# An empty planned step between a reciprocal and the scaling that reads it, with new ranks, in a planned attention and MLP-Mixer kernel

## The chip, the cores and the metric

The kernel runs on one core of a Trainium2 chip. The metric is device time in microseconds of one execution, lower is better. The profile is one execution seen by the hardware profiler; its times count from the first instruction.

## The reference

Top-32 attention for 8 batches of 8 heads, 576 rows, 64 columns a head, and behind it a token- and channel-mixing MLP. What is computed:

```python
scores = scale * np.matmul(q, k.transpose(0, 1, 3, 2))
kth = np.partition(scores, -top_k, axis=-1)[..., -top_k:-top_k + 1]
scores = np.where(scores >= kth, scores, -1000000000.0)
scores = scores - np.max(scores, axis=-1, keepdims=True)
attn = np.exp(scores)
attn = attn / (np.sum(attn, axis=-1, keepdims=True) + 1e-09)
x = np.matmul(attn, v)                      # heads laid side by side: 576 x 512 a batch
u = x + (np.maximum(x.T @ w_tok1, 0) @ w_tok2).T
out = u + np.maximum(u @ w_ch1, 0) @ w_ch2
```

## The kernel before

Work is cut into 32 units; a unit is one pair of heads of one batch, so four units make a batch. A unit's scores are nine tiles of 128 rows by 576 columns, in two groups: group 0 has four tiles, group 1 five.

**Through the engines.** TensorE makes scores, ScalarE copies them to SBUF (`SS`). VectorE finds the 32nd largest value of each row: `upper` (L428) takes the larger of two halves, `split4` (L452, L456, L460) halves again, `top_round` runs MAX8 and MATCH_REPLACE8 in rounds (L473, L478), and `low_round` (L492) ends the search. GpSimd meanwhile makes the smaller halves by integer arithmetic (`both_bits` L435, `lower_bits` L443). From the result, `raise_kth` (L544) makes `kbig`, which ScalarE needs for a steep ReLU (L550); GpSimd's `sink` (L558) subtracts it from the scores, and ScalarE's exponential follows (L532); those tiles are turned by DMA transposes (L563). The other tiles are turned on TensorE (L582, L585). In the last group of the last unit VectorE masks directly (`kept`, L574).

**Output of the attention.** For each head (`hh` 0 or 1), TensorE multiplies by v with a column of ones beside it (`o_mm`, L650), so that the row sums come out as a 65th column. VectorE takes their reciprocal (`o_den`, L662). Then the product is scaled: on ScalarE in five pieces (`o_ev`, L672), or on VectorE in one instruction (`o_ev_dve`, L681). `DIVIDED = (0, 1)` gives VectorE the second head of every odd unit, so 16 scalings, one of them in the last unit. `h1_mm` (L692) and what follows it use the scaled result.

**The last batch.** Partial sums of the MLP's second part are made on TensorE early (`pre_mm`, L1103) and copied out, one by ScalarE and eleven by VectorE (L338). When the last unit's attention is done, the rest is added to them (L1174, L1178) and the output accumulated (L1156). VectorE also checks flags: seven parts (L1253), a reduction (L1256) and a cast (L1263).

**The order.** All of this is put down as steps of a planner (`Plan`, L40). A step has an engine, a planned duration, a priority, the steps that it depends on, the buffers that it takes and gives back, and a slack: a planned time that must pass behind its predecessor on another engine. `Plan.order` plays the steps through in planned time; whenever an engine is free it takes, of the steps that are ready, the one with the lowest priority number. Steps marked as using the port (all of GpSimd's arithmetic, and VectorE's `upper` and `split4`) aren't started while another such step runs. What comes out is only an order: each engine executes its instructions in it, and waits for data by semaphores. Priorities are 100 per unit plus an entry of `RANK` for most kinds of step. Three entries are no priorities but times in tenths of a microsecond: `o_wait` (ahead of a reciprocal, behind the output matmul), `t_wait` (behind a DMA transpose) and `q_wait` (ahead of the transposes of q and k). A step on the pseudo engine "FREE" takes no time and issues nothing; what depends on it becomes ready 0.12 us (`LAG` of VectorE) behind a VectorE step that it depends on, where a VectorE step that depends on it directly would be ready at once. `raise_kth` has had such a step ahead of it already.

Of the kernel before, what the change touches and what calls it, by code (L numbers as in the profile page):

```python
# [17 lines left out]
JOINT = 4  # L18
PRE_OF = 12
RANK = {  # L20
    "begin_l": -2054, "o_wait": 16, "t_wait": 6, "q_wait": 272, "v_wait": 112, "pre_mm": -34365, "pre_ev": -31279, "rest_mm": 14920,
    "begin": 31546, "flags": 8794, "rush": -6145, "rush6": -3394, "load": -9078, "qk_tr": 7627, "qk_ev": -3163, "st_mm": -8007,
    "st_ev": 896, "keep": 3463, "h1_mm": -30213, "h1_ev": 3666, "ut_mm": -46945, "ut_ev": -3088, "out_mm": 13329, "out_ev": -772,
# [5 lines left out]
}  # L29
SPARE_US = 0.22  # L30
LEAD = 3.0
# [8 lines left out]
class Plan:  # L40
# [9 lines left out]
    def add(self, eng, dur, prio, fn, deps=(), acq=(), rel=(), slack=0.0, port=None):  # L50
        t = Task()
        t.eng, t.dur, t.prio, t.fn, t.acq, t.rel, t.slack = eng, dur, prio, fn, acq, rel, slack
        t.succ, t.nd, t.ready, t.seq = [], 0, 0.0, len(self.tasks)
        t.port = (eng == "POOL") if port is None else port
        for d in deps:
            if d is not None:
                d.succ.append(t)
                t.nd += 1
        self.tasks.append(t)
        return t  # L60
# [88 lines left out]
def kernel(  # L149
# [494 lines left out]
    def o_mm(st, mst, p, hh, wide=False):  # L644
        PT = st["PT"]
        O = bank("mps" if wide and hh else "O")[:, 0 : NS * D1].rearrange("p (t d) -> p t d", t=NS)
        for t in range(NS):
            ms = csz(t)
            for j in range(NS):
                nc.tensor.matmul(  # L650
                    out=O[0:ms, t, :],
                    lhsT=PT[:, hh, j, t * P : t * P + ms],
                    rhs=mst["vb"][:, j, 2 * p + hh, :],
                    start=(j == 0),
                    stop=(j == NS - 1),
                )
        st["O", hh] = O

    def o_den(st, hh):
        O = st["O", hh]  # L660
        rden = denp.tile([P, NS], f32, name="rden", tag="rden")
        nc.vector.reciprocal(rden[:, :], O[:, :, D])  # L662
        st["rden", hh] = rden

    def o_ev(st, mst, hh, p):
        if "Xb" not in mst:
            mst["Xb"] = take("xb", xbufs)
        Xb, O, rden = mst["Xb"], st.pop(("O", hh)), st["rden", hh]
        c0 = (2 * p + hh) * D
        for t in range(NS):  # L670
            ms = csz(t)
            nc.scalar.activation(  # L672
                out=Xb[0:ms, t, c0 : c0 + D],
                in_=O[0:ms, t, 0:D],
                func=AF.Copy,
                scale=rden[0:ms, t : t + 1],
            )

    def o_ev_dve(st, mst, hh, p):
        O, c0 = st.pop(("O", hh)), (2 * p + hh) * D  # L680
        nc.vector.tensor_tensor(  # L681
            out=mst["Xb"][:, :, c0 : c0 + D], in0=O[:, :, 0:D],
            in1=st["rden", hh][:, :].unsqueeze(2).to_broadcast([P, NS, D]), op=ALU.mult,
        )
# [129 lines left out]
    add = pl.add  # L814
# [41 lines left out]
    def plan_unit(u):  # L856
        b, p = divmod(u, NPAIR)
        st, mst = sts[u], msts[b]
        U = 100 * u
        last = u == NU - 1  # L860
# [8 lines left out]
        for i in range(2):  # L869
# [5 lines left out]
                    deps=[a] + (ev[-1:] if u else []), rel=[("tp", u, "q", i)])  # L875
# [8 lines left out]
        kd, selE, keep, nmx, PTd = {}, {}, {}, {}, {}  # L884
# [4 lines left out]
        for g in range(2):  # L889
# [6 lines left out]
            for hh in range(2):  # L896
# [3 lines left out]
                        deps=[a] + ([] if early else evs),  # L900
# [14 lines left out]
            if g == 1:  # L915
                for part in range(2):
                    a = add("PE", (1.01, 0.28)[part], U + RANK["st_mm"], lambda part=part: st_mm(st, part),
                            deps=[smm[-1]], acq=[("s0", u, "st", part)],
                            rel=[("qkT", u)] if part else [])
# [3 lines left out]
                            deps=[a, e0] + ([evs[-1]] if part else []),  # L923
                            rel=[("s0", u, "st", part)])
# [34 lines left out]
        def to_pt(t):  # L959
            return [t, home], []  # L960

        tails = []
        for g in range(2):
# [4 lines left out]
            for i in gtiles(g):  # L968
                if i in st["turned"]:
# [11 lines left out]
                    deps, acq = to_pt(y)  # L981
# [14 lines left out]
                deps, acq = to_pt(tr)  # L996
# [3 lines left out]
                rel=[(f"SS{g}", u), ("nmax", u, g)]  # L1000
# [3 lines left out]
            for tiles in [pairs] + [[i] for i in olds if i not in pairs]:  # L1004
                if not tiles:
                    continue
                tr = add("PE", 0.14 + (0.055 if fast else 0.105) * len(tiles), V + RANK["pt_tr" + str(g)] + 4 * g, lambda tiles=tiles: ptail_tr(st, tiles),
                         deps=mains, acq=[("tp", u, "l", tiles[0])],
                         rel=[(r, u, i) for r in ("E" if fast else "EU") for i in tiles])
                deps, acq = to_pt(tr)  # L1010
                tails.append(
                    add("ACT", 0.07 + 0.1 * len(tiles), V + RANK["pt_ev" + str(g)], lambda tiles=tiles: ptail_ev(st, tiles),
                        deps=deps, acq=acq, rel=[("tp", u, "l", tiles[0])])
# [4 lines left out]
        oe, oes = None, []  # L1018
        for hh in range(2):
            wide = last and hh  # L1020
            div = wide or hh >= 2 - DIVIDED[u % 2]
            O = ("mps" if wide else "O", u, hh)
            om = add("PE", 1.01, V + RANK["o_mm" + str(hh)], lambda hh=hh: o_mm(st, mst, p, hh, last),
                     deps=[wt["v", b, t] for t in range(NS)] + [None if last else oe] + tails + [PTd[i] for i in range(NTILE) if i == 2 * NT or i % 2 == hh],
                     acq=[O], rel=([("PT", u)] if hh else []) + ([("vb", b)] if hh and p == NPAIR - 1 else []))
            r = add("DVE", 0.08, U - 500, lambda hh=hh: o_den(st, hh), deps=[om], acq=[("den", u, hh)],
                    slack=0.0 if last else (0.3 if b == B - 1 else 0.1 * RANK["o_wait"]))
            if div:
                oe = add("DVE", 0.53, U - 500, lambda hh=hh: o_ev_dve(st, mst, hh, p), deps=[r], rel=[O, ("den", u, hh)])
            else:  # L1030
                oe = add("ACT", 0.99, V + RANK["o_ev" + str(hh)], lambda hh=hh: o_ev(st, mst, hh, p), deps=[r],
                         acq=[("Xb", b)] if p == 0 and hh == 0 else [], rel=[O, ("den", u, hh)])
            oes.append(oe)
# [9 lines left out]
        for part in range(2):  # L1043
# [4 lines left out]
                    deps=[a] + mst.get("ute", [])[:1],  # L1048
# [224 lines left out]
    for u in range(NU):  # L1273
        plan_unit(u)
        if u == NU - 2:
            plan_part_sums(B - 1)
        if u == NU - 1:
            plan_mlp_last(B - 1)
        elif (u + 1) % NPAIR == 0:
            plan_mlp(u // NPAIR)  # L1280
# [6 lines left out]
    with tc.If(flag != 0):  # L1287
        with tc.For_i(0, B, 1) as bv:
            mst = {}
            for p in range(NPAIR):  # L1290
                st = {"turned": ()}
# [82 lines left out]
```

## Time and profile before

| what | value |
|---|---|
| time, median of 3 runs | 885.52 us (884.84 to 885.58) |
| the profiled execution's own time | 884.62 us |
| its span, first to last instruction | 882.8 us |
| mean granted TensorE clock | 0.999 |
| VectorE busy | 861.7 us, 98% |
| ScalarE busy | 834.1 us, 94% |
| TensorE busy | 819.8 us, 93% |
| GpSimd busy | 597.2 us, 68% |

Of the profiled execution's time, 1.8 us lie around the span. TensorE's busy time has filler matmuls in it (L277), which keep it running where it has nothing to do. In the rows quoted below, DVE is VectorE, ACT ScalarE, PE TensorE, POOL GpSimd. A row of the timeline has the start and the duration in us, the engine, the line, the operation and its tiles, and how many instructions are merged. A row of a group has the count, then the busy time in us and the mean duration in ns, then the idle time ahead of them.

### The profile page before, as it was taken

What the parts mean: (1) busy time and instruction counts of PE and PEld (TensorE: products, weight loads), DVE (VectorE), ACT (ScalarE), POOL (GpSimd) and SP (SyncE); (2) the same over time, 40 slices, a digit from 0 to 9 for tenths busy, and PEclk for the clock granted to TensorE, in tenths of its full rate; (3) what the DMA queues carried; (4) which work ended last, traced back from release to release, by engine and by line L of the source; (5) the groups of instructions that cost most, each with busy time, mean ns of one, the idle gap of its engine ahead of it and who ended that gap; (6) DMA issues with size and microseconds to landing.
All of it is one profiled execution on the core that took longest, in us unless ns stands there. A gap on an engine that the chain in (4) does not pass through costs nothing.

```text
span 882.8 us, 22107 instructions
## 1 busy us (share of the span) xinstructions
PE 819.8 (93%) x7328; PEld 468.6 (53%) x7417; DVE 861.7 (98%) x3850; ACT 834.1 (94%) x1857; POOL 597.2 (68%) x513
## 2 busy tenths in 40 slices
PE   8998988999989999999999999899989999899997
PEld 5666545455545555455554555455555455545552
DVE  8999999999999999999999999999999999999993
ACT  4999999999999999999999999999999999999953
POOL 5679776776877766686676777577667767656700
PEclk9999999999999999999999999999999999999999
DMA  9656764254233453226432552224431453111101
GB/s 129 76 93 83 97 96 77 30 86 83 57 59 42 86 84 83 30 42 121 64 58 38 66 110 57 58 38 90 79 77 31 54 110 55 23 32 43 56 19 58
DMA packets 207483, 58.93 MB, mean 67 GB/s; under 512 B 199809, under 2 KB 202305, under 8 KB 207361
## 3 DMA queue, kind: packets, MB, share of 16 engines
q1 hardware_dynamic: 164320, 48.33, 27.2%
q0 software_dynamic: 40560, 8.46, 11.8%
q8 instruction: 60, 0.98, 0.5%
q10 hardware_dynamic: 2480, 0.66, 0.4%
q14 instruction: 63, 0.51, 0.2%
HBM read 35.78 MB, written 9.44 MB: 51 GB/s over the span
## 4 chain that ended last, share of the span: by engine, by line
ACT 52%; DVE 28%; PE 13%; issue 4%; POOL 2%; DMA 1%; SPq 0%; DVEq 0%; ACTq 0%
ACT SS L336 10%; DVE A L473 7%; ACT E L532 7%; DVE hx L478 6%; ACT U L567 6%; ACT U L550 6%; ACT pb L532 5%; PE mps L788 4%; DVE A L492 4%; ACT pt L605 4%; ACT H2T L754 4%; DVE hi L428 3%; ACT xb L672 3%; ACT qkT L336 2%; DVE hx L460 2%
## 5 line engine op out<-in xcount | busy, mean ns | idle before, releaser
L435 POOL TENSOR_TENSOR lo<-SS 128x1152 int32<-128x1152 int32 x64 | 168.8, 2638 | 241.8 <-DVE A L473 178.0
L473 DVE MAX8 A<-hx 128x8 f32<-128x72 f32 (+2 forms) x1152 | 270.1, 294 | 0.0
L478 DVE MATCH_REPLACE8 hx<-A,hx 128x72 f32<-128x72 f32 (+1 forms) x864 | 199.4, 242 | 0.0
L336 ACT COPY SS<-s 128x512 f32<-128x512 f32 x379 | 171.7, 527 | 5.5 <-PE s L389 5.2
L443 POOL TENSOR_TENSOR lo<-lo,hi 128x1152 int32<-128x1152 int32 x64 | 168.7, 2636 | 0.0
L389 PE MATMUL s<-qkT 64*128 64x512 f32 x508 | 161.6, 640 | 0.4 <-ACT SS L336 0.4
L558 POOL TENSOR_TENSOR SS<-SS,U 128x576 f32<-128x576 f32 x126 | 158.6, 1275 | 0.0
L532 ACT ACTIVATE E<-SS,nmax 128x576 bf16<-128x576 f32 x162 | 129.0, 824 | 1.8 <-POOL nmax L518 1.7
L582 PE MATMUL tp<-identB,E 128*128 128x128 bf16 (+1 forms) x785 | 117.4, 221 | 11.0 <-ACT pt L609 7.6
L567 ACT ACTIVATE U<-SS,A 128x576 bf16<-128x576 f32 x157 | 126.7, 837 | 0.0
L585 PE MATMUL tp<-identN,U 128*128 128x128 bf16 (+1 forms) x785 | 112.7, 220 | 9.9 <-ACT U L567 9.0
L492 DVE MAX8 A<-lo 128x8 f32<-128x296 f32 x288 | 116.9, 452 | 0.0
L550 ACT ACTIVATE U<-SS,kbig 128x576 bf16<-128x576 f32 x126 | 100.0, 822 | 4.0 <-DVE kbig L544 4.0
L788 PE MATMUL mps<-wc2b,H2T 128*128 128x512 bf16 (+1 forms) x402 | 101.9, 380 | 1.9 <-issue 1.4
L532 ACT ACTIVATE pb<-SS,nmax 128x576 bf16<-128x576 f32 x126 | 99.5, 814 | 4.2 <-POOL SS L558 4.0
L585 PEld LDWEIGHTS <-U 128*128 128x128 bf16 (+1 forms) x785 | 77.3, 100 | 37.0 <-ACT U L567 20.5
L428 DVE TENSOR_TENSOR hi<-SS 128x1152 f32<-128x1152 f32 x64 | 96.7, 1511 | 0.1
L582 PEld LDWEIGHTS <-E 128*128 128x128 bf16 (+1 forms) x785 | 75.9, 100 | 30.8 <-issue 20.4
L747 PE MATMUL mps<-UT,wc1b 128*128 128x512 bf16 x311 | 80.1, 380 | 6.1 <-ACT H2T L769 2.1
L605 ACT ACTIVATE pt<-tp 128x512 bf16<-128x512 f32 x130 | 79.0, 635 | 2.2 <-PE tp L580 2.2
L389 PEld LDWEIGHTS s<-qkT 64*128 64x128 f32 x508 | 50.5, 185 | 37.3 <-issue 16.4
L650 PEld LDWEIGHTS <-pt 128*128 128x128 bf16 (+1 forms) x1600 | 60.1, 100 | 19.0 <-issue 10.1
(142 smaller groups left out, 1501.2 us busy)
## 6 DMA issues: line engine op xcount, KB each, us to landing
qL<-in_q_dram SPq DMA_DIRECT2D x64, 128.0 KB, 2.7
kL<-in_k_dram SPq DMA_DIRECT2D x60, 128.0 KB, 2.6
out_dram<-ob SPq DMA_DIRECT2D x28, 256.0 KB, 2.1
vb<-in_v_dram POOLq DMA_DIRECT2D x32, 128.0 KB, 4.4
pt<-pb SPq DMA_TRANSPOSE x126, 2.9
wc1b<-in_moe_w_ch_dram POOLq DMA_DIRECT2D x4, 384.0 KB, 5.7
wc2b<-in_moe_w_ch_dram POOLq DMA_DIRECT2D x4, 384.0 KB, 6.0
qL<-in_q_dram SPq DMA_DIRECT2D x32, 32.0 KB, 2.5
```

Source lines behind the costliest of these rows:

```text
L336: nc.scalar.copy(out=out, in_=in_)
L389: nc.tensor.matmul(out=x[:, :], lhsT=T[rows[hh], 0, t * P : (t + 1) * P], rhs=T[rows[hh], 1, 0:W], start=True, stop=True,)
L435: nc.gpsimd.tensor_tensor(out=x[:, 0:4, 0:HALF].bitcast(i32), in0=SS[:, 0:4, 0:HALF].bitcast(i32), in1=SS[:, 0:4, HALF:S].bitcast(i32), op ...
L443: nc.gpsimd.tensor_tensor(out=x, in0=x, in1=st["hi"][:, 0:4, :].bitcast(i32), op=ALU.subtract)
L473: nc.vector.max(A[:, i, at], hx[:, i, 0:w])
L478: nc.vector.match_replace(hx[:, i, 0:w], A[:, i, TOP[r] : TOP[r] + 8], hx[:, i, 0:w], NEG)
L532: nc.scalar.activation(out=x, in_=srow(st, i), func=AF.Exp, bias=st["nmax", g][:, a : a + 1], scale=scale,)
L550: nc.scalar.activation(out=U[:, :], in_=srow(st, i), func=AF.Relu, bias=st["kbig", g][:, a : a + 1], scale=-STEEP,)
L558: nc.gpsimd.tensor_tensor(out=x, in0=x, in1=st["U", i][:, :], op=ALU.subtract)
L567: nc.scalar.activation(out=U[:, :], in_=srow(st, i), func=AF.Relu, bias=kcol(st, i), scale=-1.0)
L582: nc.tensor.matmul(out=out, lhsT=st["E", i][:, cols], rhs=identB[:, :], start=True, stop=False)
L585: nc.tensor.matmul(out=out, lhsT=st["U", i][:, cols], rhs=identN[:, :], start=False, stop=True)
```

## The change

For every scaling on VectorE but the last unit's, a step on "FREE" is put between the reciprocal and the scaling, and the scaling's planned duration becomes 0.43 in place of 0.53. Nothing is issued for the empty step. All entries of `RANK` get new values but `v_wait` and `begin_l`. From line 1029 on, lines of the changed kernel have a number that is higher by 2.

```diff
 RANK = {
-    "begin_l": -2054, "o_wait": 16, "t_wait": 6, "q_wait": 272, "v_wait": 112, "pre_mm": -34365, "pre_ev": -31279, "rest_mm": 14920,
-    "begin": 31546, "flags": 8794, "rush": -6145, "rush6": -3394, "load": -9078, "qk_tr": 7627, "qk_ev": -3163, "st_mm": -8007,
...
-    "sink1": -5954, "exp_t0": -3794, "exp_t1": -6073, "below0": 2165, "below1": 11963, "p_tr0": 1171, "p_tr1": -26336, "p_ev0": 5579,
-    "p_ev1": -62498, "pt_tr0": -9392, "pt_tr1": -1933, "pt_ev0": 7940, "pt_ev1": 9043, "o_mm0": 8167, "o_mm1": -17681, "o_ev0": -3137,
-    "o_ev1": -655,
+    "begin_l": -2054, "o_wait": 4, "t_wait": 0, "q_wait": 117, "v_wait": 112, "pre_mm": -32233, "pre_ev": -27577, "rest_mm": 10769,
+    "begin": 32835, "flags": 8597, "rush": -5226, "rush6": -1958, "load": -6530, "qk_tr": 5708, "qk_ev": -3298, "st_mm": -6852,
...
+    "sink1": -5988, "exp_t0": -1868, "exp_t1": -5701, "below0": 5955, "below1": 13098, "p_tr0": 1245, "p_tr1": -26413, "p_ev0": 5153,
+    "p_ev1": -64424, "pt_tr0": -5612, "pt_tr1": -3686, "pt_ev0": 11100, "pt_ev1": 8213, "o_mm0": 10300, "o_mm1": -17251, "o_ev0": -653,
+    "o_ev1": 2062,
 }
@@ plan_unit
             r = add("DVE", 0.08, U - 500, lambda hh=hh: o_den(st, hh), deps=[om], acq=[("den", u, hh)],
                     slack=0.0 if last else (0.3 if b == B - 1 else 0.1 * RANK["o_wait"]))
             if div:
-                oe = add("DVE", 0.53, U - 500, lambda hh=hh: o_ev_dve(st, mst, hh, p), deps=[r], rel=[O, ("den", u, hh)])
+                if not last:
+                    r = add("FREE", 0.0, 0, lambda: None, deps=[r])
+                oe = add("DVE", 0.53 if last else 0.43, U - 500, lambda hh=hh: o_ev_dve(st, mst, hh, p), deps=[r], rel=[O, ("den", u, hh)])
```

More of the change, by code (lines that the diff above doesn't have):

```diff
@@ L20 @@
 RANK = {
-    "begin_l": -2054, "o_wait": 16, "t_wait": 6, "q_wait": 272, "v_wait": 112, "pre_mm": -34365, "pre_ev": -31279, "rest_mm": 14920,
-    "begin": 31546, "flags": 8794, "rush": -6145, "rush6": -3394, "load": -9078, "qk_tr": 7627, "qk_ev": -3163, "st_mm": -8007,
-    "st_ev": 896, "keep": 3463, "h1_mm": -30213, "h1_ev": 3666, "ut_mm": -46945, "ut_ev": -3088, "out_mm": 13329, "out_ev": -772,
[5 rows of a table removed]
+    "begin_l": -2054, "o_wait": 4, "t_wait": 0, "q_wait": 117, "v_wait": 112, "pre_mm": -32233, "pre_ev": -27577, "rest_mm": 10769,
+    "begin": 32835, "flags": 8597, "rush": -5226, "rush6": -1958, "load": -6530, "qk_tr": 5708, "qk_ev": -3298, "st_mm": -6852,
+    "st_ev": -2458, "keep": 5393, "h1_mm": -28160, "h1_ev": 5916, "ut_mm": -45474, "ut_ev": -4520, "out_mm": 12928, "out_ev": 1591,
[5 rows of a table added]
 }
```

4 rows, old and new, of the table RANK are left out of this document.

## The prediction

> **What bounds the kernel.** I read the page's busy line first, then VectorE's waits, then the timeline around the instructions that the change touches.
>
> ```profile
> span 882.8 us, 22107 instructions
> PE 819.8 (93%) x7328; PEld 468.6 (53%) x7417; DVE 861.7 (98%) x3850; ACT 834.1 (94%) x1857; POOL 597.2 (68%) x513
> DVE hx L1199 <- PE s L1156: 6.0, 1, 6.0
> L681 DVE TENSOR_TENSOR xb<-O,rden 128x320 bf16<-128x320 f32 x15 | 7.4, 492 | 0.5
> ```
>
> VectorE is busy 861.7 of 882.8 us. Its longest wait, 6.0 us, is for the closing matmuls; none of its waits on another engine lies between the first few microseconds and the last unit. So VectorE sets the pace, and an edit is worth what it does to the start-to-start times on VectorE, and to the tail, where TensorE and ScalarE finish what VectorE feeds. L681 is the scaling that the change moves, fifteen times before the last unit.
>
> Now the pair itself, in the timeline (start, duration):
>
> ```profile
> 90.72 0.45 DVE L460 TENSOR_TENSOR hx<-lo 128x288 f32<-128x288 f32 x1
> 91.09 0.19 DVE L662 RECIPROCAL rden<-O 128x5 f32<-128x5 f32 x1
> 91.31 0.49 DVE L681 TENSOR_TENSOR xb<-O,rden 128x320 bf16<-128x320 f32 x1
> 91.72 0.63 DVE L473 MAX8 A<-hx 128x8 f32<-128x72 f32 x4
> ```
>
> The reciprocal starts 0.08 before L460 ends, and MAX8 starts 0.08 before the scaling ends: that is how neighbours stand when the second doesn't read what the first wrote. The scaling, which reads the reciprocal, starts 0.03 after it ends. A dependent neighbour thus costs 0.03 + 0.08 = 0.11 us, and that is the whole prize: 15 x 0.11 = 1.65 us. This size fits the new planned cost (0.43 for 0.53).
>
> **Part 1: the spacing.** The built program's order on VectorE tells what the empty step really does. In 12 of the 15 units something now stands between reciprocal and scaling (a MAX8 round, the L460 pair, the low round). In three (units 19, 23, 27) the plan found nothing else ready, and both stand side by side as before. Gain: 12 x 0.11 = -1.32.
>
> The Trainium skill speaks against this term: "VectorE: DVE Perf Modes", section "The DRAIN you can't avoid", says that the engine empties its pipe after each operation and that a semaphore between two operations costs nothing extra. By that rule the 0.11 would be 0 here and wherever I use it below, and the sum would end 0.2 us higher. The row disagrees: 0.03 after the end against 0.08 before it.
>
> **Part 2: kbig.** The new ranks turn another pair round. These are the end of the low round (L492), kbig (L544) and `upper` (L428) in two even units and one odd unit:
>
> ```profile
> 124.06 1.27 POOL L558 TENSOR_TENSOR SS<-SS,U 128x576 f32<-128x576 f32 x1
> 124.27 0.82 DVE L492 MAX8 A<-lo 128x8 f32<-128x296 f32 x2
> 125.12 0.23 DVE L544 TENSOR_SCALAR kbig<-A 128x4 f32<-128x4 f32 x1
> 125.27 1.73 DVE L428 TENSOR_TENSOR hi<-SS 128x1440 f32<-128x1440 f32 x1
> 126.93 0.45 DVE L452 TENSOR_TENSOR lo<-SS 128x288 f32<-128x288 f32 x1
> ...
> 149.91 1.27 POOL L558 TENSOR_TENSOR SS<-SS,U 128x576 f32<-128x576 f32 x1
> 150.27 1.20 DVE L492 MAX8 A<-lo 128x8 f32<-128x296 f32 x3
> 151.38 1.64 DVE L428 TENSOR_TENSOR hi<-SS 128x1440 f32<-128x1440 f32 x1
> 152.94 0.16 DVE L544 TENSOR_SCALAR kbig<-A 128x4 f32<-128x4 f32 x1
> 153.01 0.45 DVE L452 TENSOR_TENSOR lo<-SS 128x288 f32<-128x288 f32 x1
> ...
> 278.45 2.52 POOL L558 TENSOR_TENSOR SS<-SS,U 128x576 f32<-128x576 f32 x2
> 280.91 1.73 DVE L428 TENSOR_TENSOR hi<-SS 128x1440 f32<-128x1440 f32 x1
> ```
>
> In the odd unit (second group) kbig comes after `upper` and reads nothing fresh: no gap, 0.07 us. After the change every odd unit has kbig ahead of `upper`, as the even one has. There kbig reads what the last MAX8 wrote: MAX8 ends at 125.09, kbig starts at 125.12, a dependent neighbour again. In ten odd units it now follows the low round directly and pays +0.11 (10 x 0.11 = +1.10); in five the scaling, now moved there, stands between, and it pays nothing. Its own slot, 0.08 ahead of `upper` for 0.07 behind it, is a wash.
>
> Does GpSimd's sink then catch `upper`, as in the even units? There `upper` starts 0.06 before the sink ends (125.27 against 125.33, 280.91 against 280.97) and lasts 1.73 for 1.64: it is held until GpSimd lets go, and a reciprocal put in ahead of it is free (the third group has two ahead, the first one). In the odd unit the sink ends at 151.18 and `upper` starts at 151.38. With the spacing won and kbig ahead it starts at 151.38 - 0.11 + 0.11 + 0.08 = 151.46, still clear, so I count 0; caught in all fifteen it would cost 15 x 0.09 = 1.35.
>
> **Part 3: other reciprocals.** Two of them leave the even units' free places for stretches where they cost their slot, 0.09 each (row at 554.42 below): +0.2. Middle of the kernel: -1.32 + 1.10 + 0.2 = 0.0, between -1.3 (kbig's gap hidden) and +1.35 (`upper` caught).
>
> **Part 4: the tail.** Here the new ranks move most. Below are `kept` (L574), copies of the partial sums (L338), flag parts (L1253), TensorE's partial sums (L1103) and output matmuls (L650):
>
> ```profile
> 839.94 2.27 DVE L574 SCALAR_TENSOR_TENSOR E<-SS,A,E 128x576 bf16<-128x576 f32 x3
> 842.12 1.29 DVE L338 COPY SS<-mps 128x512 f32<-128x512 f32 x2
> 843.32 0.81 DVE L574 SCALAR_TENSOR_TENSOR E<-SS,A,E 128x576 bf16<-128x576 f32 x1
> 844.04 1.29 DVE L338 COPY SS<-mps 128x512 f32<-128x512 f32 x2
> 845.24 0.81 DVE L574 SCALAR_TENSOR_TENSOR E<-SS,A,E 128x576 bf16<-128x576 f32 x1
> 847.17 0.67 DVE L1253 TENSOR_TENSOR hi<-ends 128x288 f32<-128x288 f32 x1
> 847.75 1.28 DVE L338 COPY SS<-mps 128x512 f32<-128x512 f32 x2
> 848.50 1.47 PE L1103 MATMUL mps<-UT,wc1b 128*128 128x512 bf16 x6
> 849.80 1.04 PE L650 MATMUL O<-vb,pt 128*128 128x65 bf16 x25
> 851.30 0.20 DVE L662 RECIPROCAL rden<-O 128x5 f32<-128x5 f32 x1
> 851.43 1.06 PE L650 MATMUL mps<-vb,pt 128*128 128x65 bf16 x25
> 852.57 0.20 DVE L662 RECIPROCAL rden<-mps 128x5 f32<-128x5 f32 x1
> 852.80 0.49 DVE L681 TENSOR_TENSOR xb<-mps,rden 128x320 bf16<-128x320 f32 x1
> 854.91 1.05 DVE L1256 TENSOR_REDUCE flagged<-hi 128x1 f32<-128x864 f32 x1
> 856.34 0.15 DVE L1263 CAST flagged<-mps 1x1 int32<-1x1 f32 x1 [0.37 <-PE mps L1260]
> ```
>
> VectorE has no idle time here: the first kept plus pair round lasts 844.04 - 842.12 = 1.92, which is two copies of 0.60 and a kept of 0.72. The seventh copy frees the bank for L1103 at 848.50; from there TensorE runs without pause to the last output matmul (852.49), the reciprocal waits for it (852.57), and the scaling at 852.80 releases the last unit's MLP. Ahead of that seventh copy stand five kept, one flag part (0.58, from 847.17 to 847.75) and six copies; of the other six flag parts three come before the scaling, and three with the reduction after it, where the matmuls hide them.
>
> After the change five kept come first, then a flag part ahead of every pair of copies: four flag parts ahead of the seventh copy, and all seven ahead of the last scaling. Three more at 0.58 put the seventh copy at 848.35 + 1.75 = 850.10. TensorE's order from there is the same, so the last scaling moves by +1.75. Behind the scaling flags fall away from VectorE, but it wasn't late there: its cast at 856.34 waited for a matmul. The orders after the scaling are the same otherwise. I take +1.75. Bounds: 0, were the flag parts to fill waits for TensorE's banks, and +2.3, should the first partial sums on TensorE come late too, since two score transposes and two evictions now go ahead of them.
>
> **Part 5: shorter planned waits.** `o_wait` falls from 1.6 to 0.4 us, `t_wait` from 0.6 to 0. A reciprocal blocks VectorE's whole queue if its matmuls aren't done:
>
> ```profile
> 551.40 1.05 PE L650 MATMUL O<-vb,pt 128*128 128x65 bf16 x25
> 554.42 0.17 DVE L662 RECIPROCAL rden<-O 128x5 f32<-128x5 f32 x1
> 554.51 1.32 DVE L428 TENSOR_TENSOR hi<-SS 128x1152 f32<-128x1152 f32 x1
> DMA to landing us min/median/max: 2.6/2.9/6.9
> ```
>
> This margin is 554.42 - 552.45 = 1.97; less 1.2 leaves about 0.77. A late DMA transpose (up to 6.9 for a median of 2.9) could use it up. An estimate from these rows: one stall in each of eight batches, 0 to 0.4 us, so 0 to 3; I take 0.2, nearest to the margin row. `q_wait` falls from 27.2 to 11.7, still above the 6.9 of any transpose, so 0. On the DMA queue transposes and stores change places; VectorE meets them only through these reciprocals. GpSimd's order is unchanged. The start is unchanged: the first forty ScalarE instructions and the first VectorE groups stand in the same order.
>
> **Sum.** 0.0 + 1.75 + 0.2 = +1.95 on the profiled execution's 884.62 us: 886.6. That execution lies 0.90 below the median of 885.52, so on the median's scale it is 887.5. About 0.2% (1.77 us) is what a measurement of this kernel can tell from no change; the forecast lies just past it.
>
> **Rivals.**
> A, not slower: in the tail the flag parts fill waits for TensorE's two banks. For it: without a filler a pair takes 1.2 us on VectorE, less than two partial sums of three matmuls on TensorE (1.47 for the six). Against it: with a filler the round is VectorE's sum exactly. It decides if VectorE shows idle time between the copies after the change. Time: 885.52 + 0.2 = 885.7, or 884.4 with the middle's -1.3. Chance 0.30.
> B, more slower: reciprocals stall VectorE at the thin margins, or the sinks catch `upper` in odd units: +1 to +3 on top, 888.5 to 890.5. For it the late transposes; against it margins of 0.5 and more. Chance 0.16.
> C, the edit does what it says and nothing else counts: 15 gaps saved, tail hidden: 885.52 - 1.65 = 883.9, and below it if the tail is shorter too. Against it are three pairs left as they were and ten new kbig gaps. Chance 0.06.
> The forecast (886.5 to 888.5) has 0.48.
>
> **Numbers.** Predicted 887.5, the forecast's own. The range takes in A's upper time and most of B: 885.2 to 889.6. Slower by over 0.2% (above 887.29) are B and some two thirds of the forecast: 0.16 + 0.32 = 0.48. Faster (below 883.75) is about C with a little of A: 0.08. The rest is 0.44.
>
> **What would show it.** Right: twelve scalings start before their predecessor's end, kbig starts 0.03 after a MAX8 in ten odd units, `upper` there lasts 1.64, the last low round ends within 0.5 us of 840.03, and the last scaling starts near 854.5. Wrong: VectorE waiting before a reciprocal or a copy, `upper` at 1.73 in odd units, or a last scaling at 852.8.

## The result, and the profile after

| | before | after |
|---|---|---|
| time, median of 7 runs each, same chip | 885.23 us (884.55 to 885.58) | 887.91 us (887.18 to 888.57) |
| ratio after to before | | 1.0032 (1.0023 to 1.0041) |
| profiled execution, own time and span | 884.62, 882.8 | 887.18, 885.4 |

The change costs 2.7 us, between 2.0 and 3.6. The forecast was 887.5. First the busy line on the page of the changed kernel:

```profile
span 885.4 us, 22104 instructions
PE 810.8 (92%) x7326; PEld 468.5 (53%) x7416; DVE 862.1 (97%) x3850; ACT 834.3 (94%) x1857; POOL 594.2 (67%) x513
```

Three of VectorE's waits in it, all in the tail (total us, times, longest):

```profile
DVE hx L1201 <- PE s L1158: 6.0, 1, 6.0
DVE flagged L1265 <- PE mps L1262: 2.0, 1, 2.0
...
DVE rden L662 <- PE mps L650: 0.2, 1, 0.2
```

Two of its groups, by shape (count, busy us and mean ns of one, idle us ahead of them):

```profile
L681 DVE TENSOR_TENSOR xb<-O,rden 128x320 bf16<-128x320 f32 x15 | 7.2, 480 | 0.1
L544 DVE TENSOR_SCALAR kbig<-A 128x4 f32<-128x4 f32 x32 | 7.8, 245 | 0.6
```

VectorE's busy time is the same within 0.4 us (861.7 before), and it still waits for no engine in the middle. The idle time ahead of the fifteen scalings fell from 0.5 to 0.1 us: three of them still stand 0.03 or 0.04 behind their reciprocal, twelve start 0.07 to 0.09 before their neighbour's end. Its timeline shows one of the twelve, with the reciprocal gone from its side, and then kbig in an odd unit.

```profile
90.35 0.81 DVE L460 TENSOR_TENSOR hx<-lo 128x288 f32<-128x288 f32 x2
91.09 0.48 DVE L681 TENSOR_TENSOR xb<-O,rden 128x320 bf16<-128x320 f32 x1
91.49 0.62 DVE L473 MAX8 A<-hx 128x8 f32<-128x72 f32 x4
...
150.02 1.18 DVE L492 MAX8 A<-lo 128x8 f32<-128x296 f32 x3
151.24 0.23 DVE L544 TENSOR_SCALAR kbig<-A 128x4 f32<-128x4 f32 x1
151.38 1.65 DVE L428 TENSOR_TENSOR hi<-SS 128x1440 f32<-128x1440 f32 x1
152.95 0.45 DVE L452 TENSOR_TENSOR lo<-SS 128x288 f32<-128x288 f32 x1
```

kbig starts 0.04 after the MAX8 ends, where `upper` stood before, and `upper` lasts 1.65: not held. What can be held is kbig itself. In this trace every kbig of four columns that lasts longer than 0.17 us ends 0.03 after the end of a GpSimd operation (0.20 to 0.33 us, the one above 0.23). The longest is in unit 22, and `upper` starts late behind it:

```profile
592.05 0.56 DVE L544 TENSOR_SCALAR kbig<-A 128x4 f32<-128x4 f32 x1
592.53 1.64 DVE L428 TENSOR_TENSOR hi<-SS 128x1440 f32<-128x1440 f32 x1
```

The tail in the same timeline, VectorE first, then TensorE's first partial sums:

```profile
840.28 3.71 DVE L574 SCALAR_TENSOR_TENSOR E<-SS,A,E 128x576 bf16<-128x576 f32 x5
843.91 0.66 DVE L1255 TENSOR_TENSOR hi<-ends 128x288 f32<-128x288 f32 x1
844.49 1.28 DVE L338 COPY SS<-mps 128x512 f32<-128x512 f32 x2
845.69 0.67 DVE L1255 TENSOR_TENSOR hi<-ends 128x288 f32<-128x288 f32 x1
846.26 1.30 DVE L338 COPY SS<-mps 128x512 f32<-128x512 f32 x2
...
849.83 1.28 DVE L338 COPY SS<-mps 128x512 f32<-128x512 f32 x2
854.59 0.20 DVE L662 RECIPROCAL rden<-mps 128x5 f32<-128x5 f32 x1 [0.20 <-PE mps L650]
854.82 0.49 DVE L681 TENSOR_TENSOR xb<-mps,rden 128x320 bf16<-128x320 f32 x1
878.73 0.42 DVE L1191 COPY ob<-tp 64x256 f32<-64x256 f32 x1 [0.73 <-ACT ob L1189]
842.48 2.39 PE L1105 MATMUL mps<-UT,wc1b 128*128 128x512 bf16 x9
```

Five kept in a row, then rounds of a flag part and two copies. The last scaling starts at 854.82 (852.80 before).

The following table cuts every profiled execution at four instructions of VectorE: the first `upper`, the first `kept` of the tail, the last scaling, and the last copy of the output. "Middle" runs from the first to the second, "tail" to the third, "end" to the fourth, "close" to the end of the span.

| kernel | middle | tail | end | close | its time | median of runs | median of before beside it |
|---|---|---|---|---|---|---|---|
| before | 829.41 | 12.86 | 23.96 | 6.04 | 884.62 | 885.23 | |
| after | 829.82 | 14.54 | 23.91 | 6.67 | 887.18 | 887.91 | 885.23 |
| scalings moved only | 827.83 | 12.85 | 23.94 | 6.42 | 883.84 | 883.77 | 884.98 |
| flag parts ahead only | 829.21 | 14.54 | 23.91 | 6.07 | 886.90 | 886.51 | 884.98 |
| empty step only | 829.30 | 16.71 | 24.39 | 6.54 | 889.67 | 890.42 | 884.98 |
| ranks only | 830.61 | 13.81 | 24.48 | 6.44 | 887.71 | 887.76 | 884.98 |
| after, flag parts back | 829.59 | 14.19 | 23.93 | 6.86 | 886.94 | 887.05 | 884.85 |
| after, kbig back | 828.73 | 15.00 | 23.91 | 6.76 | 886.79 | 888.22 | 884.85 |
| the same again | 829.55 | 15.01 | 23.92 | 6.88 | 888.33 | 888.33 | 885.23 |
| after, both back | 828.82 | 14.85 | 23.94 | 6.96 | 887.32 | 888.26 | 884.85 |
| scalings moved, flags last | 828.54 | 12.07 | 26.73 | 6.58 | 886.98 | 886.01 | 884.85 |
| after, tail back | 829.20 | 13.48 | 23.94 | 6.26 | 885.30 | 886.27 | 885.23 |
| after, waits back | 830.32 | 14.55 | 23.91 | 6.32 | 887.36 | 888.16 | 885.23 |
| after, kbig and tail back | 829.84 | 13.49 | 23.94 | 6.21 | 886.34 | 886.34 | 885.23 |

So of the 2.6 us of span, 1.68 lie in the tail and 0.41 in the middle. The other 0.63 lie behind the last copy, where both kernels have only the same output stores left. That stretch takes 6.04 to 6.58 in the profiles with the old ranks and 6.21 to 6.96 in those with the new ones; whether it belongs to the change stays open.

The middle is one execution each, and it varies. Profiles whose order of VectorE is the same up to the first `kept` differ by 0.2 (before, and flag parts ahead; after, and flag parts back), by 0.7 (scalings moved only, and with flags last) and by 0.8 (kbig back, twice). The two large differences are mostly holds by GpSimd: 0.55 of the 0.70 and 0.51 of the 0.82 lie between the start of a kbig and the start of the step behind it.

### The profile page after: what moved, and what is told of

Read it like the earlier page. It is cut to its first block, busy times and chain, and to the rows that moved or that the text cites. A ratio compares the mean times of both kernels' runs of the same rounds, so it can differ in the third digit from the quotient of the medians.

```text
span 885.4 us, 22104 instructions
## 1 busy us (share of the span) xinstructions
PE 810.8 (92%) x7326; PEld 468.5 (53%) x7416; DVE 862.1 (97%) x3850; ACT 834.3 (94%) x1857; POOL 594.2 (67%) x513
## 4 chain that ended last, share of the span: by engine, by line
DVE 52%; ACT 29%; PE 9%; POOL 4%; issue 4%; ACTq 0%; DVEq 0%
DVE A L473 14%; DVE hx L478 12%; DVE A L492 7%; DVE hi L428 6%; ACT SS L336 5%; ACT E L532 4%; ACT U L567 3%; DVE lo L456 3%; DVE hx L460 3%; DVE hx L456 3%; ACT U L550 3%; ACT pb L532 2%; ACT pt L605 2%; ACT xb L672 2%; POOL lo L435 2%
## 5 line engine op out<-in xcount | busy, mean ns | idle before, releaser
L389 PE MATMUL s<-qkT 64*128 64x512 f32 x508 | 155.3, 641 | 0.7 <-ACT SS L336 0.7
L532 ACT ACTIVATE pb<-SS,nmax 128x576 bf16<-128x576 f32 x126 | 103.3, 833 | 5.2 <-POOL SS L558 5.1
L550 ACT ACTIVATE U<-SS,kbig 128x576 bf16<-128x576 f32 x126 | 102.4, 837 | 0.4 <-DVE kbig L544 0.4
L605 ACT ACTIVATE pt<-tp 128x512 bf16<-128x512 f32 x130 | 82.3, 655 | 3.3 <-PE tp L580 2.3
L650 PE MATMUL O<-vb,pt 128*128 128x65 bf16 x1575 | 66.1, 195 | 5.4 <-ACT xb L672 5.2
```

The lines of the kernel that those rows point to most:

```text
L389: nc.tensor.matmul(out=x[:, :], lhsT=T[rows[hh], 0, t * P : (t + 1) * P], rhs=T[rows[hh], 1, 0:W], start=True, stop=True,)
L532: nc.scalar.activation(out=x, in_=srow(st, i), func=AF.Exp, bias=st["nmax", g][:, a : a + 1], scale=scale,)
```

## The experiments

In the experiments that move steps in the finished plan, steps get a tag and the plan is rearranged before it is issued, so that nothing else moves; their line numbers are higher by 6 to 13.

**The scalings alone.** Kernel before, each of the fifteen scalings behind VectorE's next step.

```diff
-        for _, t in self.order():
+        plan = [t for _, t in self.order()]
+        for t in [x for x in plan if getattr(x, "tag", "") == "scale"]:
+            i = plan.index(t)
+            j = next(n for n in range(i + 1, len(plan)) if getattr(plan[n], "eng", "") == "DVE")
+            plan.insert(j, plan.pop(i))
+        for t in plan:
```

> The kernel before; only each of the fifteen scalings is put behind the next planned VectorE step, every other instruction stands where it stood. Theory (a dependent neighbour starts 0.11 us later than an independent one): 15 x 0.11 = 1.65 us less, 883.6 for 885.2; in the trace no scaling starts 0.03 after its reciprocal's end. Rival (the pipe is emptied after each instruction anyway, so that it costs nothing to depend on the neighbour): 885.2. A middle value, 884.4, would mean that part of the won time is lost again where GpSimd's sink holds `upper`.

Measured: 883.77 for 884.98, ratio 0.9985 (0.9976 to 0.9994); the middle is 1.58 shorter in this profile (0.87 in the later run that has the same order up to the first `kept`). This version beats both kernels. The scalings' group by shape:

```profile
L687 DVE TENSOR_TENSOR xb<-O,rden 128x320 bf16<-128x320 f32 x15 | 7.2, 477 | 0.0
```

Two rows of its timeline, a scaling and a reciprocal near the end of the middle:

```profile
93.01 0.48 DVE L687 TENSOR_TENSOR xb<-O,rden 128x320 bf16<-128x320 f32 x1
...
829.10 0.20 DVE L668 RECIPROCAL rden<-O 128x5 f32<-128x5 f32 x1 [0.47 <-PE O L656]
```

No scaling has a gap left. From the end of L460 to the next `upper` each odd unit became shorter by 0.166 us (2.49 over fifteen), more than the 0.11 of the gap: the scaling is 0.015 shorter, and a MAX8 beside a reciprocal 0.03 shorter than beside a scaling. Of the 2.49, some 0.6 came back in the odd units' second groups, where `upper` meets the sink more often (mean 1.67 for 1.65), and 0.47 where VectorE, now early, waits for output matmuls (829.10). Dependence on the neighbour has a price; the rival that puts it at nothing is out.

**The flag parts alone.** Kernel before, flag parts at other places: behind the 2nd, 4th, 6th (two), 8th and 10th copy and behind the reciprocal.

```diff
+        flags = [x for x in plan if getattr(x, "tag", "") == "flag"]
+        plan = [x for x in plan if x not in flags]
+        at = [x for x in plan if getattr(x, "tag", "") in ("copy", "den", "last")]
+        for x, n in reversed(list(zip(flags, (1, 3, 5, 5, 7, 9, 10)))):
+            plan.insert(plan.index(at[n]) + 1, x)
```

> The kernel before; only flag parts are moved: four stand ahead of the seventh partial-sum copy (one before), all seven ahead of the last scaling. Theory (in the tail VectorE's sum sets the time, flag parts included): 3 x 0.58 = 1.75 us more, 887.0, and the last scaling at 854.5 in the trace. Rival A of the prediction (the flag parts fill waits for TensorE's two banks): 885.2 to 885.7, the last scaling near 852.8 to 853.3.

Measured: 886.51 for 884.98, ratio 1.0019 (1.0010 to 1.0028); the tail is 1.68 longer. Three rows of its timeline, the 5th to 8th copy:

```profile
847.77 1.28 DVE L345 COPY SS<-mps 128x512 f32<-128x512 f32 x2
848.97 1.25 DVE L1263 TENSOR_TENSOR hi<-ends 128x288 f32<-128x288 f32 x2
850.13 1.28 DVE L345 COPY SS<-mps 128x512 f32<-128x512 f32 x2
```

Copies and flag parts follow each other without a wait. In the order of before, flag parts ahead cost their full time.

**Each half of the change alone.** The empty step and the 0.43 with the old ranks, and the new ranks without the step.

> The empty step and the planned 0.43 alone, with the old ranks. By the order that the planner then writes, twelve pairs are separated (-1.32), nine more kbig stand right behind the low round (+0.99), and in the tail seven flag parts, the reduction and one reciprocal stand ahead of the seventh copy, for one flag part before: 6 x 0.58 + 0.97 + 0.2 = +4.65. Theory: +4.3, 889.5. With the tail's fillers hidden: 884.9. If dependence costs nothing but the tail counts: 889.9.

> The new ranks and the shorter planned waits alone, without the empty step. All pairs stay together, thirteen kbig (fourteen before) stand right behind the low round (-0.11), two flag parts stand ahead of the seventh copy, one before (+0.58). Theory, with 0.2 for two reciprocals and 0.2 for the shorter waits: +0.9, 886.1. Rival B (reciprocals stall VectorE where the planned wait is short): +1 to +3 on top, 887 to 889, with waits of VectorE for TensorE in the middle of the trace. If the flag part is hidden: 885.5.

Measured: 890.42 (ratio 1.0063, 1.0049 to 1.0076) and 887.76 (1.0032, 1.0020 to 1.0044). The step alone came out as expected in kind: the seventh copy starts 12.41 after the first kept for 7.81 before, +4.60 for the 4.65 counted (0.30 of it is a wait for TensorE that I hadn't counted); the last scaling is then 3.85 later and the end 0.43 longer. The ranks alone cost as much as the whole change, and my +0.9 was too low: the middle is longer by 1.20, not 0.3. Ten reciprocals (two before) stand in the odd units' second groups, ahead of an `upper` that nothing holds: 8 x 0.09 = 0.72 (0.75 measured there); units 3 and 5, where a pair moved ahead of the split and kbig ahead of `upper`, are longer by 0.29 each. No reciprocal waited there, so rival B isn't the reason. With the step the middle is 0.79 shorter again. The tail counted two flag parts (0.58) and is 0.95 longer.

**Flag parts, kbig, and both, put back in the changed kernel.** For kbig, tagged in the odd units:

```diff
+        for t in [x for x in plan if getattr(x, "tag", "") == "kbig"]:
+            i = plan.index(t)
+            j = next(n for n in range(i + 1, len(plan)) if getattr(plan[n], "eng", "") == "DVE")
+            if plan[j].tag == "upper":
+                plan.insert(j, plan.pop(i))
```

The edit reaches one unit further than "back": it moves sixteen kbig, unit 1's too, which the kernel before has ahead of `upper` just as the changed one does.

> The changed kernel; only the flag parts go back to where the kernel before has them (one ahead of the seventh copy, three behind the last scaling). Theory: the 1.75 of the tail comes back, less what six copies in a row lose to TensorE, whose partial sums take 0.73 per bank for VectorE's 0.60 (4 x 0.13 = 0.5): 1.2 to 1.75 less than the changed kernel's 887.9, so 886.2 to 886.7, the last scaling 1.2 to 1.7 earlier after the first `kept` than in the changed kernel. Rival A (flag parts fill waits): no more than 0.6 less, 887.3 or above, with VectorE waiting for TensorE before most copies.

> The changed kernel; only kbig goes back behind `upper` in the odd units. Theory: ten of them stood 0.03 behind the end of a MAX8 and lose that gap, 10 x 0.11 = 1.1 less, 886.8; in the trace `upper` in odd units then comes 0.19 earlier after the low round and is held a little by the sink (1.67 for 1.66, as where the scalings alone were moved). Rival (dependence costs nothing): 887.9.

> The changed kernel with both put back, flag parts and kbig. If the two terms are separate, the sum of the two: 2.3 to 2.85 less than the changed kernel, 885.0 to 885.6; that is the kernel before with twelve gaps saved and the remaining changes of order against it. Rival (the gains are won in the same wait, so that they don't add up): no better than the better one of the two alone, 886.2 to 886.8.

Measured: 887.05 (ratio 1.0025, 1.0016 to 1.0035), 888.22 (1.0048, 1.0032 to 1.0063) and 888.26 (1.0046, 1.0031 to 1.0061). All three missed. The flag parts gave back 0.35 of the tail's 1.68, and the timeline says why: VectorE now waits for TensorE before the copies. Its timeline, three pairs of VectorE's copies and three rows of TensorE:

```profile
844.75 0.69 DVE L345 COPY SS<-mps 128x512 f32<-128x512 f32 x1 [0.18 <-PE mps L1114]
845.62 1.41 DVE L345 COPY SS<-mps 128x512 f32<-128x512 f32 x2 [0.18 <-PE mps L1114]
847.43 1.34 DVE L345 COPY SS<-mps 128x512 f32<-128x512 f32 x2 [0.40 <-PE mps L1114]
840.82 0.39 PE L720 MATMUL mps<-w2b,H1T 128*128 128x512 bf16 x1 [0.62 <-ACT H1T L711]
841.57 0.61 PE L587 MATMUL tp<-identB,E 128*128 128x128 bf16 x8
842.32 2.39 PE L1114 MATMUL mps<-UT,wc1b 128*128 128x512 bf16 x9
```

The same two matmuls in the timeline of the kernel before:

```profile
837.88 0.41 PE L713 MATMUL mps<-w2b,H1T 128*128 128x512 bf16 x2
...
839.90 2.29 PE L1103 MATMUL mps<-UT,wc1b 128*128 128x512 bf16 x9 [0.25 <-ACT UT L737]
```

TensorE's first partial sums start at 842.3 to 842.5 here and in the changed kernel, at 839.90 before. In the new order they stand behind the transposes that need the first kept (L587 here), and behind a product with H1T that comes 3 us later. So the tail has two causes side by side, and either alone costs most of it: 1.68 with the flag parts ahead in the order of before, 1.33 here with the partial sums late. With kbig back the middle is shorter by 1.09 in this profile; 0.46 of it is lost again in the tail to the same partial sums. What the medians add on top is the subject of the runs with kbig back further down.

**The tail put back on both engines.** The changed kernel with the old `pre_mm`, `pre_ev`, `pret_mm`, `pret_ev`, `rush` and `rush6`, and the flag parts at their old places.

> The changed kernel with the old ranks for the partial sums and for the hurry of the last two batches, and with the flag parts where the kernel before has them: TensorE then starts its partial sums ahead of the transposes of the last scores, as before. Theory, after putting the flag parts alone back brought 0.35 in the trace for 1.75: in the changed kernel two things run side by side in the tail, VectorE's four flag parts and TensorE's partial sums, which begin 2.6 later, and either alone costs all of it. With both put back the last scaling comes 12.9 to 13.2 after the first `kept` (14.54 in the changed kernel, 12.86 before): 1.3 to 1.7 less, 886.2 to 886.6. Rival (the kept steps in one row cost it): no more than the 0.35, 887.5.

Measured: 886.27, ratio 1.0013 (1.0004 to 1.0022), 1.6 below the changed kernel. From its timeline, TensorE's first partial sums and the last scaling:

```profile
840.16 2.29 PE L1114 MATMUL mps<-UT,wc1b 128*128 128x512 bf16 x9
...
853.10 0.49 DVE L688 TENSOR_TENSOR xb<-mps,rden 128x320 bf16<-128x320 f32 x1
```

The partial sums start 2.3 earlier (1.7 when counted from the first `kept`) and the tail takes 13.48, so 1.06 of the 1.68 are back. The other 0.62 isn't taken apart: four kept stand ahead of the first copy, for three before, the partial sums still start 0.6 later after the first `kept`, and one copy waits 0.3. So flag parts on VectorE and late partial sums on TensorE cost it together: of the tails of before, of flag parts ahead only, of flag parts back and of this kernel, the two with early sums and late flag parts are short.

**The planned waits put back.** `o_wait` 16, `t_wait` 6, `q_wait` 272 in the changed kernel.

> The changed kernel with the old planned waits (o_wait, t_wait, q_wait) and nothing else: the plan then leaves reciprocals 1.6 us after their matmuls again; three more kbig stand behind a low round. Theory (the short waits cost 0.2, the gaps 3 x 0.11): no change within 0.2 of the changed kernel, 887.7 to 888.1. Rival B (short waits stall VectorE in some executions): the median falls by 0.5 or more, below 887.4, and the times lie closer together.

Measured: 888.16 (ratio 1.0031, 1.0020 to 1.0043), between 886.99 and 888.28; its middle is 0.5 longer, with 0.33 counted for three more kbig. The short waits cost nothing that can be measured here.

**kbig back with the old tail, and kbig back once more.**

> The changed kernel with kbig behind `upper` again in the odd units and the tail as in the run with the old tail. If both terms add up: 1.1 + 1.5 less than the changed kernel, 885.3. Rival (with kbig back the reciprocals' margins are so thin that VectorE stalls in some executions, as the spread of 886.8 to 892.0 with kbig alone put back suggests): a fastest time near 885.0, but a median of 886.5 or more and a spread of 3 us.

> The changed kernel with kbig alone put back once more, for a second profile and more times. If the first run's spread (886.8 to 892.0) is the kernel's own: again a spread of 3 us or more, and, should a slow execution be profiled, waits of VectorE's reciprocals for output matmuls that make up the difference. If it was the chip at that moment: times within 1 us, around 886.8.

Measured: 886.34 (884.89 to 889.70) and 888.33 (886.81 to 891.63): the spread is the kernels' own. With the tail back too the sum (885.3) was missed, and the rival came near: the fastest time is 884.89, the spread 4.8, the median 886.34 for its 886.5 or more. The second profile of kbig alone back has the clock at 0.998 and no reciprocal that waits longer than 0.13; its middle is 0.82 longer than the first one's by GpSimd's holds (0.51 at kbig, 0.21 at `upper`).

The profiled execution of the first fell on a longer one, 1.45 above its fastest. VectorE's second longest wait in it:

```profile
DVE rden L674 <- PE O L662: 1.4, 1, 1.4
```

The reciprocal that waited, in the timeline:

```profile
63.45 0.20 DVE L674 RECIPROCAL rden<-O 128x5 f32<-128x5 f32 x1 [1.36 <-PE O L662]
```

One wait of 1.36 is nearly the whole difference. TensorE was late. Stretches of that execution (us, busy time and count of each engine in the order PE, PEld, DVE, ACT, POOL; the third number from the end is the granted clock):

```profile
48.00:50.00 2.00, 0.66 (x2) 0.00 (x0) 2.00 (x4) 1.16 (x3) 2.00 (x3) 1.00 0.53 106
50.00:52.00 2.00, 1.72 (x14) 0.97 (x15) 2.00 (x4) 2.00 (x6) 0.27 (x1) 0.98 0.82 87
52.00:54.00 2.00, 2.00 (x12) 0.96 (x9) 2.00 (x18) 1.93 (x4) 1.69 (x1) 0.50 0.87 167
54.00:56.00 2.00, 2.00 (x10) 0.55 (x8) 2.00 (x17) 1.09 (x3) 2.00 (x3) 0.67 0.03 8
```

The first of these stretches in the changed kernel:

```profile
48.00:50.00 2.00, 1.35 (x4) 0.29 (x2) 2.00 (x3) 2.00 (x6) 1.81 (x2) 1.00 0.61 124
```

And in the kernel before:

```profile
48.00:50.00 2.00, 1.64 (x4) 0.35 (x3) 2.00 (x3) 2.00 (x6) 1.90 (x2) 1.00 0.58 116
```

ScalarE does less in that stretch (1.16 of 2.00 us), and TensorE, which waits for its evictions, has 1.34 idle, for 0.65 in the changed kernel and 0.36 before. What ScalarE waits for is the kbig of unit 1, the one that the edit moved beyond the order of before:

```profile
49.30 0.78 ACT L562 ACTIVATE U<-SS,kbig 128x576 bf16<-128x576 f32 x1 [0.84 <-DVE kbig L556]
```

Then TensorE's clock fell to a half, for 3.4 us by the last three stretches (0.08 + 2.00 + 1.32). The idle time doesn't always bring this about. With kbig alone back, the first profile has the same stretch with the clock at 1.00, there and four microseconds later:

```profile
48.00:50.00 2.00, 0.64 (x2) 0.00 (x0) 2.00 (x4) 1.16 (x3) 2.00 (x3) 1.00 0.54 109
52.00:54.00 2.00, 2.00 (x15) 0.70 (x12) 2.00 (x18) 2.00 (x5) 1.71 (x1) 1.00 0.85 168
```

The spread goes with the granted clock: in the four runs with kbig back, the nine executions with a mean clock of 0.995 or less took 888.78 to 892.14 us, those with 0.997 or more 884.89 to 888.60 (four at 0.996, the profiled one among them, 886.34 to 886.85). None of the nine was profiled, so where their clock fell isn't shown. At 0.997 or more the kernel with kbig and tail back took 885.08 in the median of five, 1.2 below the one with the tail alone back, about the 1.1 counted for kbig. In the other two pairs the gain isn't there: kbig alone back took 887.75 in the median of eight, 0.2 below the changed kernel, and with the flag parts back too 887.32 in the median of three, 0.3 above the one with the flag parts alone back. The Trainium skill, "TensorE: Matmul & The Clock Gate", Part 1, tells of a gate that halves the clock by TensorE's activity in a window of about 3.4 us that runs free of the kernel. The rows agree in depth (0.50) and length (3.4). A free-running window would also explain why the same idle time is followed by a half clock in one execution and not in another; no row here shows the window itself.

**The candidate from these.** The scalings moved, as in the first run, and the flag parts and the reduction behind the last joins, by one more dependence on the join (`deps=[a, j]`).

> The kernel before with the fifteen scalings behind the next planned VectorE step, and the seven flag parts and the reduction behind the last joins, where VectorE waits 6 us for the closing matmuls. Theory: 1.2 less for the scalings, as measured for them alone, and 0.58 less for the one flag part that stood ahead of the seventh copy: 883.2 for 885.0. Rivals: TensorE's banks set the copies' pace once the fillers are gone: 883.6 to 883.8; the late flag matmul holds up the closing matmuls on TensorE's queue: 884 to 885.

Measured: 886.01 for 884.85, ratio 1.0013 (1.0004 to 1.0021): no rival had it. Three rows of its timeline, the last unit's scaling and reciprocal and the first join:

```profile
851.79 0.49 DVE L687 TENSOR_TENSOR xb<-mps,rden 128x320 bf16<-128x320 f32 x1
852.54 0.20 DVE L668 RECIPROCAL rden<-O 128x5 f32<-128x5 f32 x1 [0.26 <-PE O L656]
858.54 0.42 DVE L1185 TENSOR_TENSOR SS<-O,SS 128x256 f32<-128x256 f32 x1 [5.80 <-PE O L769]
```

The tail is 0.79 shorter, but not like for like. Without the flag parts the planner also turned the last unit's two halves round: the first head's reciprocal, at 851.30 before and ahead of the other, now comes after the last scaling. ScalarE's scaling behind it starts late, the first join begins at 858.54 (856.56 before), and the end is 2.77 longer.

## Why the prediction was right, and where it wasn't

**VectorE sets the pace**: it held, apart from the places where GpSimd holds a step of VectorE. The stretches of VectorE explain the result to 0.6 us.

**Part 1, the spacing.** Right in number: twelve pairs apart, three not. The price of a pair was too small, 0.166 for 0.11 where nothing catches it, but part of that is given back to the sink and to TensorE. The measured 1.58 for fifteen would make 1.26 for twelve, for the 1.32 predicted; that they are so close is partly luck, since a larger price and a part lost again cancel. The rule that I weighed against it, from the Trainium skill's "VectorE: DVE Perf Modes" (a semaphore between two operations costs nothing extra), did not hold in the first run, where the pairs set apart saved 2.49 between L460 and `upper`. The same section of the Trainium skill, "The DRAIN you can't avoid", also says that an operation that isn't held starts earlier; the -0.08 agrees with that.

**Part 2, kbig.** The gap was right: eighteen kbig start 0.03 or 0.04 behind a MAX8, ten of them in odd units that had no gap before, and `upper` in odd units lasts 1.64 to 1.66 in thirteen of fifteen cases. With kbig alone back, eleven gaps are gone in both profiles. The middle is shorter by 1.09 in the first and by 0.27 in the second, for the 1.10 counted, so the size of the term in time is not settled. I had watched only `upper` for GpSimd's hold; kbig is caught as well. Its slot of 0.08 holds in eleven of the fifteen odd units where it moved, the other four take 0.12 to 0.20. The idle time at 48 to 52 us belongs to the experiment, which moved unit 1's kbig as well.

**Part 3, other reciprocals.** Mis-sized: I counted two. In the odd units' second groups alone two became six (4 x 0.09 = 0.36), and that stretch, from the last split to `upper`, grew by 0.63. And in unit 22 a reciprocal and the held kbig made the stretch from one `upper` to the next 0.34 longer; my "a reciprocal put in ahead of it is free" did not hold there in this execution. (In the profile with the flag parts back, which has the same order, that kbig is hardly caught: 0.15 from its start to `upper`, for 0.48.) The middle came out at +0.41 for the +0.2 of parts 1 to 3 and 5; the last low round ends 0.34 later, within the 0.5. With 0.2 to 0.8 between profiles of one order, that nearness is luck in part.

**Part 4, the tail.** The number was right, 1.68 for 1.75 (854.82 for the 854.5 named), the cause half of it. VectorE has no wait between the copies, so its own steps set the time, as counted. But the partial sums on TensorE start 2.6 later too, and the flag parts mostly fill a wait for them that would be there without the flag parts: these alone give back only 0.35. I had named late partial sums, as something on top (up to +2.3); they run beside. That two delays of nearly the same size overlap and don't add is luck for the number.

**Part 5, shorter waits.** Within the 0.2: putting them back changed nothing measurable, and no reciprocal waited in the middle of the changed kernel.

**Sum.** +1.95 predicted on the profiled execution; its stretches give +0.41 + 1.68 - 0.05 = +2.04, and 0.6 in the close and the start, whose cause isn't shown. **Rivals.** A is refuted as a time, but its mechanism is at work inside the changed kernel, where the flag parts alone are worth only 0.35. B didn't happen in the changed kernel; a reciprocal did stall VectorE in one profiled execution with kbig back, by way of the clock. C is refuted by the three pairs, ten kbig and the tail.

## What to carry over

Two engines can be late by the same amount at the same place; undoing one of them then shows next to nothing, and only a second experiment that undoes the other tells that the first was real. An experiment that undoes something must be held against the order that it is to restore: here one step too many was moved, and that step left ScalarE and TensorE idle. A change to a planner's costs is a change to every order that it writes: most of this one's time came from ranks, and the 1.2 us of the idea itself appeared only when the steps were moved by hand in the finished plan. Where a kernel's executions spread, list the granted clock of each of them before looking for a wait.

## What the hardware showed that was not expected

- A pair of dependent neighbours on VectorE cost 0.166 us against the same two set apart, not only the visible gap of 0.11: the scaling took 477 ns for 492 when apart, and the MAX8 behind a reciprocal 0.60 for the 0.63 behind a scaling.
- A short VectorE step can be held by GpSimd: kbig, four columns, lasts 0.16 or 0.17 us, and up to 0.56 in the changed kernel where GpSimd is at work; it then ends 0.03 after GpSimd's operation. Most of the 0.7 and 0.8 by which middles of one order differ comes from this.
- TensorE, idle for 1.34 of 2 us, was granted half its clock some 2 us later, and four matmuls of the scores took 2.08 us for 1.13; in another execution the same idle time left the clock at 1.00. The 1.36 us that VectorE lost by it came at a reciprocal that had no room left: with kbig alone put back and the clock at 1.00, the step ahead of it ends at 61.86 and it starts at 61.99, a wait of 0.13 already.
